# Attention with routed and dense MLPs: value tiles with places of their own in the plan, first loads put ahead of the decay sums

## The chip, the cores and the metric

One core of a Trainium2 chip runs the whole program. The metric is the device time of one execution in microseconds, as a median over runs; the profile is one further execution, recorded by the hardware profiler, with its own time beside it.

## What is computed

The reference, cut to what matters here: causal attention over 4 batches of 8 heads, 576 positions and 64 columns a head, with a decay that is a running sum of `max(s, 0)`; its output is the input of a top-1 mixture of 8 experts, and that of a dense two-layer network.

```python
scores = scale * np.matmul(q, k.transpose(0, 1, 3, 2))
cum = np.cumsum(np.maximum(s, 0.0), axis=-1)
bias = -(cum[:, :, :, None] - cum[:, :, None, :])
scores = np.where(causal, -1000000000.0, scores + np.minimum(bias, 0.0))
attn = np.exp(scores - np.max(scores, axis=-1, keepdims=True))
attn = attn / (np.sum(attn, axis=-1, keepdims=True) + 1e-09)
attn_out = np.matmul(attn, v)                  # then rows of 8 x 64 = 512
y = gate_w * (np.maximum(x @ w1[e], 0) @ w2[e])  # e: the expert of a row's largest logit
h = y @ w_in; out = (h * np.clip(h + 3, 0, 6) / 6) @ w_out
```

## The kernel before

**Parts in time.** The attention part comes first, then ten passes of expert products, then the dense network in steps. All three are one instruction stream for each engine. Only the attention part is touched by the change.

**Attention.** A unit is one block of 128 queries of one batch (the fifth block of a batch has 64), a pair is two heads of a unit. 80 pairs run one after the other in a software pipeline: in one slot, TensorE makes the scores of the next pair (`sp`, L575), VectorE adds the decay and finds the minimum (`ne`, L588), ScalarE takes the exponential (`pp`, L594), TensorE turns the pair before (`pt`, L603), ScalarE and VectorE split it into two float16 halves (`hi`, L624, and `lo`, L625), and TensorE multiplies the pair before that with the value tile (`o`, L658). A full unit has four pairs with two exponentials each, the fifth unit of a batch four pairs with one, so a batch has 36 exponentials.

**Inputs of a batch.** q and k come in three chunks of 256, 256 and 64 positions (`load`), are lined up by GpSimd (`xs`), turned by TensorE (`pk`, L490) and split. Values come as five tiles of 128 positions (`load_v`: two DMAs of 128 KB, into `v32`, of which there are two buffers). `v_part` makes the two halves of a value tile: a copy by ScalarE (L514), a scaling and a subtraction by GpSimd (L445 and L516), into `vbuf[b % 2][j]`; the buffers of batch b are those of batch b - 2. The decay sums `cum` are made once for all batches in 32 rows (L395 to L405), written to DRAM (`cum_d`, L407), and read back spread over 128 partitions (`load_cum`, tile `cp`). For heads 0 to 3 of the first unit, TensorE spreads the sums instead (`first_cum`, tile `pf`).

**What sets the order.** All loads are issued by SyncE (SP), one after the other; a load that waits for a buffer holds back all that stand behind it. `then` chains the first loads in the written order. Everything later is put into slots of the pair pipeline by `at_time`, on a scale where a pair costs 1.0 to 2.9 (`price`); the whole plan is 158.4 units long. For each chunk a due time is worked out backwards (`due`), and all its work is put there: the loads of its value tiles at the start, then the turns of k and q, then its value parts. Inside each engine a scheduler places an instruction by its own model of when the operands are there; `issue_after` fixes that one instruction is behind another.

**What else uses the engines there.** From batch 2 on, the first expert weights are loaded through the same staging buffers (`wf`, in turn in the `k32` and `q32` buffers) and split by GpSimd and ScalarE (L249 to L251). After a unit its rows are split (`xw`, L687 and L688) and stored (`x_d`, L690 and L695), and after a batch its tokens are scattered (`tok_d`, L804). `fold_cum` (`cp`, L445) copies sums for the fifth units and for the last batch.

## Time and profile before

| what | value |
|---|---|
| median of 3 runs | 871.22 us (870.36 to 875.09) |
| profiled execution, its own time | 872.09 us |
| its span from first to last instruction | 870.3 us |
| TensorE busy in the span | 794.4 us (91%) |
| ScalarE, GpSimd busy | 461.7 us, 296.4 us |
| ScalarE waiting for value tiles | 15.2 us up to 70 us, 4.2 us up to 140, 1.8 us up to 200 |
| last value products of the attention | at 272 us |

The span runs from the first to the last instruction; the 1.8 us between it and the execution's time lie around it. The profiled execution is 0.9 us above the median.

### The profile page before, as it was taken

The numbers are of one execution on the slowest core, as the hardware profiler recorded it, in microseconds if no ns is written. First come the engines' busy times: TensorE is split into PE (matmuls) and PEld (weight loads), VectorE is DVE, ScalarE is ACT, GpSimd is POOL, SyncE is SP. The second block draws the span as 40 slices with busy tenths as digits, with TensorE's granted clock in tenths as the row PEclk, the third lists the DMA queues.
The fourth block names the chain that finished last, engine by engine and source line by source line (L and its number), as shares of the span: only waits on it lengthen the run. The fifth ranks groups of instructions, "written<-read, shape, count | busy, mean of one in ns | idle before, by whom it ended". The sixth has DMA issues, their size and how long they took to land.

```text
span 870.3 us, 21871 instructions
## 1 busy us (share of the span) xinstructions
PE 794.4 (91%) x8340; PEld 659.7 (76%) x8340; DVE 623.5 (72%) x1542; ACT 461.7 (53%) x854; POOL 296.4 (34%) x402
## 2 busy tenths in 40 slices
PE   5888788888888998899999999999999999999993
PEld 4567567666667897566778888888888888888882
DVE  4677777866767645789879569988677777777770
ACT  3677767867875433666656343554444344443440
POOL 2565663868984225044331100000022022211232
PEclk8799999999999999999999999999999999999997
DMA  7957245243613678988887355654444545444420
GB/s 165 262 130 214 70 89 180 51 96 101 178 47 79 171 209 219 321 304 273 256 259 270 98 170 165 220 174 158 141 148 129 159 150 162 142 141 153 153 95 27
DMA packets 154327, 142.03 MB, mean 163 GB/s; under 512 B 68710, under 2 KB 122214, under 8 KB 153446
## 3 DMA queue, kind: packets, MB, share of 16 engines
q1 hardware_dynamic: 150422, 130.50, 50.2%
q0 software_dynamic: 3792, 10.06, 3.5%
q8 instruction: 67, 1.10, 0.5%
q14 instruction: 46, 0.38, 0.2%
HBM read 106.70 MB, written 28.54 MB: 155 GB/s over the span
## 4 chain that ended last, share of the span: by engine, by line
PE 48%; DMA 17%; DVE 10%; POOL 7%; ACT 5%; issue 5%; SPq 4%; another core or an unknown queue 1%; POOLq 0%; ACTq 0%; DVEq 0%
PE bank L1350 18%; PE py L1241 8%; PE bank L1267 8%; PE ph L1130 7%; DMA wf<-in_moe_w_dram 5%; DMA v<-in_v_dram 3%; PE pt L603 2%; PE sp L575 2%; PE o L658 2%; DVE wo L1110 2%; DMA t_d<-cl 2%; DMA xsT<-xg 1%; DMA t_d<-sets 1%; ACT pp L594 1%; SPq L215 1%
## 5 line engine op out<-in xcount | busy, mean ns | idle before, releaser
L1267 PE MATMUL bank<-x2T,wi 128*128 128x256 f16 x1728 | 193.5, 273 | 0.9 <-POOL x2T L1249 0.6
L1267 PEld LDWEIGHTS <-wi 128*128 128x128 f16 x1728 | 169.1, 98 | 21.0 <-issue 1.5
L1350 PE MATMUL bank<-wo,sets 128*128 128x256 f16 x1512 | 170.2, 273 | 1.2 <-DVE sets L1279 0.7
L1350 PEld LDWEIGHTS <-sets 128*128 128x128 f16 x1512 | 147.7, 98 | 19.0 <-DVE sets L1279 1.0
L1278 ACT ACTIVATE sets<-back 128x896 f16<-128x896 f32 x72 | 68.1, 950 | 91.9 <-PE bank L1350 74.7
L1130 PE MATMUL ph<-xsT,t 128*128 128x224 f16 (+7 forms) x960 | 109.6, 276 | 3.6 <-DVE hT L1135 3.6
L1241 PE MATMUL py<-hT,t 128*128 128x224 f16 (+7 forms) x960 | 108.4, 273 | 4.2 <-DVE hT L1135 2.3
L1361 POOL TENSOR_TENSOR u<-sa 128x256 f32<-128x256 f32 x9 | 9.3, 1035 | 296.4 <-ACT sa L1360 296.4
L1130 PEld LDWEIGHTS <-t 128*128 128x128 f16 x960 | 86.8, 99 | 24.1 <-issue 4.2
L1241 PEld LDWEIGHTS <-t 128*128 128x128 f16 x960 | 85.5, 98 | 25.7 <-issue 5.7
L1279 DVE SCALAR_TENSOR_TENSOR sets<-back,sets 128x896 f16<-128x896 f32 x72 | 80.2, 1119 | 22.1 <-ACT sets L1278 21.9
L625 DVE SCALAR_TENSOR_TENSOR lo<-pt,hi 128x256 f16<-128x256 f32 (+3 forms) x144 | 72.8, 519 | 28.5 <-ACT hi L624 27.4
L257 DVE SCALAR_TENSOR_TENSOR t<-wf,t 128x1024 f16<-128x1024 f32 x53 | 66.7, 1258 | 28.6 <-ACT t L254 27.9
L658 PE MATMUL o<-v,hi 128*128 128x65 f16 (+2 forms) x960 | 63.0, 201 | 24.9 <-ACT hi L624 17.9
L603 PE MATMUL pt<-idf,pp 128*128 128x128 f32 (+1 forms) x400 | 77.9, 310 | 7.5 <-DVE kT L499 1.9
L624 ACT ACTIVATE hi<-pt 128x256 f16<-128x256 f32 (+3 forms) x144 | 64.1, 460 | 35.4 <-PE pt L603 27.0
L594 ACT ACTIVATE pp<-ne,nm 128x128 f32<-128x128 f32 (+4 forms) x144 | 76.9, 580 | 0.6 <-DVE nm L588 0.6
L254 ACT ACTIVATE t<-wf 128x1024 f16<-128x1024 f32 x53 | 55.5, 1053 | 36.1 <-DMA wf<-in_moe_w_dram 36.1
L588 DVE CUSTOM_DVE_ANT_0 ne<-sp,cp 128x128 f32<-128x128 f32 (+4 forms) x144 | 61.2, 456 | 16.5 <-ACT pp L594 11.4
L658 PEld LDWEIGHTS <-hi 128*128 128x128 f16 (+2 forms) x960 | 47.9, 104 | 32.3 <-ACT hi L624 21.0
L603 PEld LDWEIGHTS pt<-idf,pp 128*128 128x128 f32 (+1 forms) x400 | 46.9, 152 | 17.5 <-issue 3.6
L1249 POOL TENSOR_TENSOR x2T<-y,x2T 128x360 f32 (+5 forms) x24 | 20.8, 871 | 111.1 <-ACT x2T L1248 97.4
(206 smaller groups left out, 1263.4 us busy)
## 6 DMA issues: line engine op xcount, KB each, us to landing
wf<-in_moe_w_dram SPq DMA_DIRECT2D x64, 512.0 KB
back<-t_d SPq DMA_DIRECT2D x144, 128.0 KB
wd<-in_moe_w_in_dram SPq DMA_DIRECT2D x16, 512.0 KB
wd<-in_moe_w_out_dram SPq DMA_DIRECT2D x16, 512.0 KB
cp<-cum_d SPq DMA_DIRECT2D x6, 1152.0 KB
t_d<-cl SPq DMA_DIRECT2D x24, 256.0 KB
t_d<-sets SPq DMA_DIRECT2D x24, 256.0 KB
t_d<-wo SPq DMA_DIRECT2D x24, 256.0 KB
```

Source lines behind the costliest of these rows:

```text
L257: stt(out=lo, in0=fv, scalar=sc, in1=hi, op0=ALU.mult, op1=ALU.subtract)
L594: mark["act"] = nc.scalar.activation(self.view(self.pp, e), self.view(self.ne, e), AF.Exp, bias=self.nm[:, e:e + 1], scale=-1.0).ins
L603: nc.tensor.transpose(self.pt[g][:m, x, :], src, idf)
L624: nc.scalar.activation(hi, pt, AF.Copy, scale=SP)
L625: stt(out=lo, in0=pt, scalar=SP, in1=hi, op0=ALU.mult, op1=ALU.subtract)
L658: mark["pe"] = nc.tensor.matmul(dst, a, x, start=first, stop=last).ins
L1130: mark["pe"] = nc.tensor.matmul(ph[:, :n], wt[c][:, a, cols], xT[:, KD * b_ + c, :n], start=(c == 0 and x == 0), stop=(c == KD - 1 and x = ...
L1241: nc.tensor.matmul(py[:, :rows], wt2[:, j_, f, cols], hT[i_][:, f, :rows], start=(f == 0 and x == 0), stop=(f == KF - 1 and x == 2),)
L1267: m = nc.tensor.matmul(dst, wi[:, a, kk, fs], x2[:, KD * b_ + kk], start=(kk == 0 and x == 0), stop=(kk == KD - 1 and x == 2),)
L1278: nc.scalar.activation(hi, t, AF.Copy, scale=SG)
L1279: stt(out=lo, in0=t, scalar=SG, in1=hi, op0=ALU.mult, op1=ALU.subtract)
L1350: m = nc.tensor.matmul(banks[k_][:, :HM], sets[:, s % 4, a, k_], w_sums[f][:, b_, k_], start=(f == 0 and x == 0), stop=(f == HO - 1 and x ...
```

## The change

It changes four things in the attention part.

- `load_v(0, 0)` and `load(0, 1)`, the first value tile and the second chunk of q and k, are issued ahead of the decay sums. The write of the sums to `cum_d` moves from SyncE's queue to ScalarE's.
- `first_cum` is called for both halves of the heads, so TensorE spreads the first 128 sums of all eight heads, and ScalarE makes two copies instead of one. The two loads of sums that opened the chain (4 heads by 256, 4 heads by 128) become one of 8 heads by columns 128 to 256.
- A value part leaves its chunk's list. `v_part` is now placed by itself: for the first two chunks of a batch behind the turns, for the third chunk at 8.5 units into its batch, and for the last batch at times of a table `v_last`, counted from the start of the batch before. Its load stands 3 units ahead of it, and its ScalarE copy is fixed behind the last exponential written before it.
- The sums of batches 1 to 3 are loaded behind the last store of rows that is written before them (`mark["x"]`).

```diff
-        with tc.issue_after(ahead[0]):
-            cum_out = nc.sync.dma_start(cum_d, cum_sb)
+        last = [ahead[0]]
+
+        def then(f, *args):
+            with tc.issue_after(last[0]):
+                last[0] = f(*args).ins
+
+        then(load_v, 0, 0)
+        then(load, 0, 1)
+        nc.scalar.dma_start(cum_d, cum_sb)
...
-        def first_cum():
+        def first_cum(h0):
...
-            pc = psT.tile([128, FIRST, 128], F32, tag="T", name="pf")
-            for h in range(FIRST):
+            pc = psT.tile([128, H // 2, 128], F32, tag="T", name="pf")
+            for h in range(H // 2):
                 nc.tensor.matmul(
-                    pc[:, h], idf[:BH, h:h + 1].to_broadcast([BH, 128]),
+                    pc[:, h], idf[:BH, h0 + h:h0 + h + 1].to_broadcast([BH, 128]),
...
-            nc.scalar.activation(cums[0][:, :FIRST, :128], pc, AF.Copy)
+            nc.scalar.activation(cums[0][:, h0:h0 + H // 2, :128], pc, AF.Copy)
...
+        def v_part(b, j):
+            def f():
+                m = R[j]
+                v32 = loaded.pop((b, j, "v"))
+                vt = vbuf[b % 2][j]
+                with tc.issue_after(mark["act"]):
+                    nc.scalar.activation(vt[:m, :, 0:D], v32[:m], AF.Copy, scale=SV)
+                hi16(v32[:m], v32[:m], SV)
+                gtt(out=vt[:m, :, D + 1:], in0=v32[:m], in1=vt[:m, :, 0:D], op=ALU.subtract)
+            return f
...
-        then(load_cum, 0, slice(FIRST, H), 0, 256)
-        then(load_cum, 0, slice(0, FIRST), 128, 256)
-        then(load_v, 0, 0)
-        then(load, 0, 1)
+        then(load_cum, 0, slice(0, H), 128, 256)
         then(load_v, 0, 1)
...
+        v_last = (4.5, 6.5, 22.0, 24.0, 26.0)
...
             at_time(t0, begin)
-            for j in range(CH[c][0] // 128, CH[c][0] // 128 + (2 if c < 2 else 1)):
-                at_time(t0, lambda b=b, j=j: load_v(b, j))
+            nt = 4 if c < 2 else 2
+            for x, j in enumerate(range(CH[c][0] // 128, CH[c][0] // 128 + (2 if c < 2 else 1))):
+                if b + 1 == B:
+                    tv = start_of(NCH * (b - 1)) + v_last[j]
+                elif c == 2:
+                    tv = start_of(NCH * b) + 8.5
+                else:
+                    tv = t0 + (nt + x) * per
+                at_time(tv - 3.0, lambda b=b, j=j: load_v(b, j))
+                at_time(tv, lambda j=j, hold=hold: hold[j]())
             at_time(t0, next_load)
...
+                    def late_cum(b=b, x=x):
+                        with tc.issue_after(mark["x"]):
+                            load_cum(b, slice(H // 2 * x, H // 2 * x + H // 2))
+
+                    at_time(t0 + x * per, late_cum)
```

The order of SyncE's queue at the start of the program, before, from the write of the sums to the third value tile (`k_223` and `q_222` are the second chunk, `v_219`, `v_226`, `v_235` the first three value tiles, `wgf` the gate's weights):

```order
L407 DMA cum_d<-cum_sb 32x576
L414 DMA cp<-cum_d 128x4x256
L414 DMA cp<-cum_d 128x4x128
L341 DMA v_219<-in_v_dram 64x8x64 x2
L329 DMA k_223<-in_k_dram 128x8x128
L329 DMA q_222<-in_q_dram 128x8x128
L341 DMA v_226<-in_v_dram 64x8x64 x2
L897 DMA wgf_101<-in_moe_w_gate_dram 128x4x8
L897 DMA wgf_102<-in_moe_w_gate_dram 64x2x8 x4
L414 DMA cp<-cum_d 128x8x320
L341 DMA v_235<-in_v_dram 64x8x64 x2
L414 DMA cp<-cum_d 128x2304 x2
```

The same stretch of SyncE's queue after the change (`v_215`, `v_225`, `v_234`, `v_237` are the value tiles 0 to 3):

```order
L341 DMA v_215<-in_v_dram 64x8x64 x2
L329 DMA k_219<-in_k_dram 128x8x128
L329 DMA q_218<-in_q_dram 128x8x128
L421 DMA cp<-cum_d 128x8x128
L341 DMA v_225<-in_v_dram 64x8x64 x2
L410 DMA wgf_101<-in_moe_w_gate_dram 128x4x8
L410 DMA wgf_102<-in_moe_w_gate_dram 64x2x8 x4
L421 DMA cp<-cum_d 128x8x320
L341 DMA v_234<-in_v_dram 64x8x64 x2
L341 DMA v_237<-in_v_dram 64x8x64 x2
```

The first value tile and the second chunk have moved to the head, and the sums of batch 1 (`128x2304 x2`, 2.36 MB) have left the place between value tiles 2 and 3.

ScalarE's order in the same stretch, before, from the fifth exponential on (the L514 rows are the copies of value tiles 0, 1 and 2):

```order
L594 ACTIVATE pp<-ne,nm 128x128
L514 ACTIVATE v_0_185<-v_219 128x8x64
L594 ACTIVATE pp<-ne,nm 128x128
L514 ACTIVATE v_1_187<-v_226 128x8x64
L498 ACTIVATE kT<-pk 128x2x256
L624 ACTIVATE hi<-pt 128x256
L594 ACTIVATE pp<-ne,nm 128x128 x2
L503 ACTIVATE xs<-pk 128x512
L624 ACTIVATE hi<-pt 128x256
L594 ACTIVATE pp<-ne,nm 128x256 x2
L514 ACTIVATE v_2_189<-v_235 128x8x64
```

ScalarE's order in the same stretch, after the change, from the first exponentials to the fourth value tile (the L458 rows are the copies of value tiles):

```order
L600 ACTIVATE pp<-ne,nm 128x128 x4
L458 ACTIVATE v_0_185<-v_215 128x8x64
L514 ACTIVATE qT<-pk 128x512
L514 ACTIVATE kT<-pk 128x2x256
L630 ACTIVATE hi<-pt 128x256 x2
L600 ACTIVATE pp<-ne,nm 128x128 x2
L458 ACTIVATE v_1_187<-v_225 128x8x64
L600 ACTIVATE pp<-ne,nm 128x128
...
L514 ACTIVATE kT<-pk 128x2x256
L630 ACTIVATE hi<-pt 128x256
L600 ACTIVATE pp<-ne,nm 128x256 x2
L458 ACTIVATE v_2_189<-v_234 128x8x64
L519 ACTIVATE xs<-pk 128x512
L458 ACTIVATE v_3_191<-v_237 128x8x64
```

Before, the copies of tiles 0, 1, 2 and 3 stood behind 5, 6, 10 and 16 exponentials; now they stand behind 4, 6, 12 and 12. Later, the five copies of batches 1 to 3 stood behind 24, 26, 30, 30 and 32; 42, 42, 50, 52 and 56; and 78, 78, 86, 88 and 92 exponentials. Now they stand behind 32, 33, 38, 42 and 52; 68, 69, 74, 78 and 88; and 82, 86, 100, 100 and 104.

GpSimd's order in batch 2, before, where the tokens of batch 1 are scattered and the first expert weights are split (`cp` is `fold_cum`, `wf` and `t` are the weight split, `xs` and `qT` belong to chunks of batch 3):

```order
L804 DMA tok_d<-what,pos_s 5120x3 x5
L445 TENSOR_SCALAR cp<-cp 64x576 x3
L249 TENSOR_SCALAR wf<-wf 128x1024
L251 TENSOR_TENSOR t_3949<-wf,t_3949 128x1024
L688 TENSOR_TENSOR xw<-xr,xw 128x512
L445 TENSOR_SCALAR xs<-k_3535 128x4x2x64
L445 TENSOR_SCALAR xs<-q_3534 128x4x2x64
L445 TENSOR_SCALAR qT<-xs 128x512
```

The same place on GpSimd after the change:

```order
L810 DMA tok_d<-what,pos_s 5120x3 x5
L450 TENSOR_SCALAR cp<-cp 64x576 x2
L450 TENSOR_SCALAR v_3696<-v_3696 128x512
L450 TENSOR_SCALAR cp<-cp 64x576
L450 TENSOR_SCALAR v_3699<-v_3699 128x512
L460 TENSOR_TENSOR v_2_199<-v_3696,v_2_199 128x8x64
L460 TENSOR_TENSOR v_3_201<-v_3699,v_3_201 128x8x64
L249 TENSOR_SCALAR wf<-wf 128x1024
L694 TENSOR_TENSOR xw<-xr,xw 128x512
L450 TENSOR_SCALAR xs<-k_3555 128x4x2x64
L450 TENSOR_SCALAR xs<-q_3554 128x4x2x64
L450 TENSOR_SCALAR v_3780<-v_3780 64x512
```

Three value parts of the last batch now stand between the scatter and the weight splits; before, they were done earlier in batch 2.

## Rows read from the trace of the kernel before

**Rows 1.** The page: span, and busy tenths and granted clock in 40 slices.

```profile
span 870.3 us, 21871 instructions
PE   5888788888888998899999999999999999999993
PEclk8799999999999999999999999999999999999997
```

**Rows 2.** ScalarE's waits (total us, times, longest), from 0:70, 70:140 and 140:200 us.

```profile
ACT v L514 <- DMA v<-in_v_dram: 15.2, 8, 4.3
...
ACT v L514 <- DMA v<-in_v_dram: 4.2, 1, 4.2
...
ACT v L514 <- DMA v<-in_v_dram: 1.8, 1, 1.8
```

**Rows 3.** Timeline of ScalarE: value tiles 0 to 2, exponentials 11 and 12.

```profile
17.60 0.64 ACT L514 ACTIVATE v<-v 128x512 f16<-128x512 f32 x1 [3.35 <-DMA v<-in_v_dram]
...
22.82 0.64 ACT L514 ACTIVATE v<-v 128x512 f16<-128x512 f32 x1 [4.29 <-DMA v<-in_v_dram]
...
31.41 0.64 ACT L514 ACTIVATE v<-v 128x512 f16<-128x512 f32 x1 [3.25 <-DMA v<-in_v_dram]
...
32.69 0.90 ACT L594 ACTIVATE pp<-ne,nm 128x256 f32<-128x256 f32 x2
```

**Rows 4.** Timeline of SyncE's issues at the start: start, us to issue, what.

```profile
7.80 0.33 SPq L407 DMA_DIRECT2D cum_d<-cum_sb  x1
9.47 0.92 SPq L414 DMA_DIRECT2D cp<-cum_d  x2
10.44 1.41 SPq L341 DMA_DIRECT2D v<-in_v_dram  x2
...
18.15 3.93 SPq L897 DMA_DIRECT2D wgf<-in_moe_w_gate_dram  x5
...
24.96 1.26 SPq L414 DMA_DIRECT2D cp<-cum_d  x2
```

**Rows 5.** Windows: length, busy PE, PEld, DVE, ACT, POOL; clock, DMA share, GB/s.

```profile
4.00:6.00 2.00, 2.00 (x7) 1.23 (x8) 1.93 (x6) 0.60 (x1) 0.18 (x1) 1.00 0.93 210
8.00:10.00 2.00, 2.00 (x16) 1.51 (x14) 0.69 (x1) 1.50 (x3) 0.00 (x0) 1.00 0.16 37
18.00:26.00 8.00, 5.32 (x38) 3.50 (x37) 1.94 (x7) 2.98 (x8) 4.29 (x8) 0.50 0.77 155
94.00:98.00 4.00, 1.37 (x19) 0.92 (x18) 1.33 (x6) 0.17 (x1) 3.46 (x10) 1.00 0.55 117
200.00:220.00 20.00, 16.06 (x268) 12.21 (x266) 12.88 (x51) 16.27 (x36) 19.47 (x21) 0.91 0.30 83
350.00:370.00 20.00, 16.61 (x105) 10.12 (x104) 16.96 (x25) 13.45 (x19) 0.00 (x0) 1.00 1.02 315
```

**Rows 6.** Waits of all engines from 92 to 104 us.

```profile
PE o L658 <- ACT hi L624: 3.8, 1, 3.8
```

**Rows 7.** Instructions on value tiles up to 275 us: ns minimum, median, maximum.

```profile
L514 ACT ACTIVATE v<-v x20: 625/637/641, 17.6 to 167.6; 128x512 f16<-128x512 f32 x16, 64x512 f16<-64x512 f32 x4
L445 POOL TENSOR_SCALAR v<-v x20: 607/617/621, 18.4 to 168.3; 128x512 f32<-128x512 f32 x16, 64x512 f32<-64x512 f32 x4
L516 POOL TENSOR_TENSOR v<-v,v x20: 1116/1127/1134, 19.8 to 169.0; 128x512 f16<-128x512 f32 x16, 64x512 f16<-64x512 f32 x4
```

**Rows 8.** Timeline of GpSimd from 185 to 200 us, its rows with idle time.

```profile
185.01 1.94 POOL L445 TENSOR_SCALAR cp<-cp 64x576 f32<-64x576 f32 x3 [4.35 <-DVE nm L588]
...
189.88 2.13 POOL L251 TENSOR_TENSOR t<-wf,t 128x1024 f16<-128x1024 f32 x1 [1.17 <-ACT t L250]
...
199.37 1.04 POOL L249 TENSOR_SCALAR wf<-wf 128x1024 f32<-128x1024 f32 x1 [2.02 <-DMA wf<-in_moe_w_dram]
```

**Rows 9.** The chain that ended last: start us, us, what.

```profile
7.80 1.65 DMA cum_d<-cum_sb
...
93.81 4.51 DMA v<-in_v_dram
...
272.46 1.64 PE o L658 x48
```

**Rows 10.** SyncE's queue up to 275 us: its longest waits in total.

```profile
SPq L690 <- POOL xw L688: 22.7, 8, 7.6
```

More of the change, by code (lines that the diff above doesn't have):

```diff
@@ L507, in turn @@
                 return [line_up, flip]
-            def v_part(j):
-                def f():
-                    m = R[j]
-                    v32 = loaded.pop((b, j, "v"))
-                    vt = vbuf[b % 2][j]
-                    nc.scalar.activation(vt[:m, :, 0:D], v32[:m], AF.Copy, scale=SV)
-                    hi16(v32[:m], v32[:m], SV)
-                    gtt(out=vt[:m, :, D + 1:], in0=v32[:m], in1=vt[:m, :, 0:D], op=ALU.subtract)
-                return f
-            vs = [v_part(t0 // 128 + j) for j in range(nr)]
+            vs = [v_part(b, t0 // 128 + j) for j in range(nr)]
             groups = ((0, 1), (2, 3)) if big else (range(NP),)
@@ L889, in start_of @@
             return begins[NP * place[u] + p]
-        last = [cum_out.ins]
-        def then(f, *args):
-            with tc.issue_after(last[0]):
-                last[0] = f(*args).ins
-        then(load_cum, 0, slice(FIRST, H), 0, 256)
-        then(load_cum, 0, slice(0, FIRST), 128, 256)
-        then(load_v, 0, 0)
-        then(load, 0, 1)
+        then(load_cum, 0, slice(0, H), 128, 256)
         then(load_v, 0, 1)
@@ L909 @@
         then(load, 0, 2)
-        at_slot(-1, first_cum)
+        for h0 in (0, H // 2):
+            at_slot(-1, lambda h0=h0: first_cum(h0))
         for x, fs in enumerate(prep(0, 0, fast=True)):
@@ L934, in begin @@
                 hold["f"] = prep(b, c)
+            hold.update((j, v_part(b, j)) for j in range(NCH))
             def next_load(g=g):
@@ L940 @@
             at_time(t0, begin)
-            for j in range(CH[c][0] // 128, CH[c][0] // 128 + (2 if c < 2 else 1)):
-                at_time(t0, lambda b=b, j=j: load_v(b, j))
+            nt = 4 if c < 2 else 2
[8 more added lines that the diff above has]
+                at_time(tv, lambda j=j, hold=hold: hold[j]())
             at_time(t0, next_load)
-            for x in range(6 if c < 2 else 3):
-                for y in range(2 if x < (4 if c < 2 else 2) else 1):
+            for x in range(nt):
+                for y in range(2):
                     at_time(t0 + (x + 1.3 * y) * per, lambda x=x, y=y, hold=hold: hold["f"][x][y]())
@@ L948 @@
                 for x in range(2):
-                    at_time(t0 + x * per, lambda b=b, x=x: load_cum(b, slice(H // 2 * x, H // 2 * x + H // 2)))
+                    def late_cum(b=b, x=x):
+                        with tc.issue_after(mark["x"]):
+                            load_cum(b, slice(H // 2 * x, H // 2 * x + H // 2))
+                    at_time(t0 + x * per, late_cum)
         def fill_tables():
```

1 line of the change is left out of this document (removed).

## The prediction

> **What bounds the kernel now.** I read the page's slices first. TensorE is at 5 to 8 tenths in the first twelve, which are the attention part, and at 8 or 9 in all behind them but the last [rows 1]; the last value products start at 272 us [rows 9]. So the expert and dense parts have little idle time to give, and the change doesn't touch them: what it is worth is how much earlier the attention part ends, and whether the rest moves up with it.
>
> In the attention part no engine is full. The pairs go round from TensorE to VectorE to ScalarE and back, and a wait of one of them for something outside the ring stops all three. The waits of ScalarE, by stretch, show such an outside wait: the copy of a value tile waits for its load for 15.2 us up to 70 us, 4.2 us up to 140 and 1.8 us up to 200 [rows 2], 21.2 us together. The timeline shows how: the copies of tiles 0, 1 and 2 stand in front of exponentials and wait 3.35, 4.29 and 3.25 us [rows 3]. That the ring stops is seen in batch 1: from 94 to 98 us ScalarE is busy for 0.17 of 4 us, TensorE for 1.37 [rows 5], and TensorE's own wait for that one stop is 3.8 us [rows 6]. The chain that ended last agrees: it runs through the write of the sums at 7.80 us and through a value load of 4.51 us at 93.81 [rows 9].
>
> Why the loads are late: SyncE issues nothing between the first q and k and the end of the sums, 7.80 us, then waits for that write to land, until 9.47 [rows 4]. From 8 to 10 us the DMA engines are busy for 0.16 of the time [rows 5]. The first value tile is issued only at 10.44, behind two loads of sums [rows 4].
>
> **The start of batch 0.** By 8 us the first q and k are in, since the DMA engines are idle then. Now the transfers can go on without the hole. Ahead of value tile 2, counted from the diff and the order, lie tile 0 (0.26 MB), the second q and k (1.05), sums (8 x 128 columns x 128 rows x 4 bytes, 0.52), tile 1 (0.26), the gate's weights, sums (8 x 320 columns, 1.31), and tile 2 itself (0.26): 3.66 MB. The 256-byte rows of the first q and k moved at 210 GB/s [rows 5]; that is 17.4 us, and I add 1 us for the gate's small rows, of whose 3.93 us of issue [rows 4] most lies beside transfers (an estimate). Tile 2 then lands at 8 + 17.4 + 1 = 26.4 us. Without the three waits, ScalarE would be through its twelfth exponential, which ended at 32.69 + 0.90 = 33.6 [rows 3], at 33.6 - 10.9 = 22.7, less the copy of tile 2 (0.6), which stood ahead of it, plus the second copy of `first_cum` (0.6, taken from the copy of a value tile, which has as many columns [rows 7]): 22.7. So it waits again, 3.7 us, for tile 2, and is through the copy at 27.0 instead of 33.6. **Gain: 6.6 us.** Tile 3 lands 1.2 us behind tile 2, and the copies of tile 2 and of `xs` fill that. The bounds: at the pace of the trace between the issue of the first sums, 9.47, and the landing of tile 1, 22.82 [rows 3, 4], 2.36 MB in 13.35 us or 177 GB/s, tile 2 lands at 29.7 and the gain is 3.3. With no wait at all it is 10.3. I take the middle one, since its row is the same kind of transfer with nothing in the way.
>
> The write of `cum_d` from ScalarE's queue costs that engine one issue, 0.33 us on SyncE [rows 4]; it stands where ScalarE waits for TensorE's first sums, so I count nothing, and the 0.33 if that cover is gone. Four more spreading products lie on TensorE in a stretch in which ScalarE has the longer work; they take the place of a load, and I count nothing (bounds: 0 and 0.6 us, one more copy's length).
>
> **The rest of batch 0.** Of the 15.2 us, 4.3 lie behind tile 2. Part of them came from the sums of batch 1 (two loads issued at 24.96 [rows 4]), which stood ahead of tile 3 and are now late. TensorE is busier here, so that some of a stop is caught up afterwards; I take half. **Gain: 2.2 us**, bounds 0 and 4.3.
>
> **Batch 1 and batch 2.** Their value tiles were copied a batch ahead, as soon as the buffers were free, with the load right ahead of the copy. Now the load stands 3 units ahead. The plan of 158.4 units ends at 272 us [rows 9], so 3 units are some 5 us, and the load took 4.51 us from issue to landing [rows 9]. That is enough, narrowly. For batch 1, I take TensorE's wait, **3.8 us** [rows 6] (bounds: 2.6, which is what TensorE lacked from 94 to 98, and 4.2); for batch 2, half of 1.8, **0.9 us** (bounds 0 and 1.8).
>
> **The last batch.** Its tiles 2, 3 and 4 move on GpSimd to behind the scatter of batch 1's tokens, among the first weight splits. Each is 0.62 + 1.13 us [rows 7], 5.2 together. GpSimd had idle time there: 4.35, 1.17 and 2.02 us [rows 8]; the first of these lies ahead of the place. Right behind it GpSimd is full, 19.47 of 20 us from 200 to 220 [rows 5], and the weight splits hold the staging buffers of the last chunks. Of the other two idle times, 3.2 us, most can hide work. I take half of the 5.2 as **loss: 2.6 us** (bounds 0 and 5.2). ScalarE's share, three copies of 0.64, is moved, not added.
>
> **The rest of the program** moves up as it is: the weight loads are put at slots of the pairs and come earlier with them. I count no loss; the price if that fails is a rival below.
>
> **Sum:** 6.6 + 2.2 + 3.8 + 0.9 - 2.6 = 10.9 us. Against the profiled execution, 870.3 of span and 1.8 around it, 872.1 - 10.9 = 861.2. That execution is 0.9 above the median of the runs shown; I forecast **861 us**, 1.2% below that median. 0.5% (4.4 us) is about what a measurement of this kernel can tell from no change: 866.9 and 875.6 are the lines.
>
> **Rivals.**
>
> *The clock holds.* From 18 to 26 us the granted clock is 0.50, the lower level of 1.2 GHz, after TensorE had stood still behind the first wait, and TensorE's 5.32 us there [rows 5] would be 2.7 at 2.4 GHz. If the early waits vanish and the clock stays up, the first term is 10.3 instead of 6.6 and 2.7 us come on top: 861 - 6.4 = 855 us. For it: the hole in the transfers is real. Against it: 3.66 MB have to come through. The Trainium skill ("TensorE: Matmul & The Clock Gate", "HAM oscillation — how this bites in real kernels") says that waits for DMA throw the array back to its half clock, and that keeping it fed avoids this; the row agrees on the fall. By that rule this rival would be the rule rather than the exception; I hold that a wait of 3.7 us remains.
>
> *The transfers bound the start.* The order changes, the bytes don't, and what waited for tile 0 and 1 now waits for the second q and k, the sums and tiles 2 and 3. At 177 GB/s the first term is 3.3, the second 0, and with GpSimd's 5.2 in full: 3.3 + 3.8 + 0.9 - 5.2 = 2.8, or 869 us.
>
> *The loads come too late (slower).* A value load is now some 5 us ahead of its copy, and ScalarE's copy can't slide behind later exponentials. In SyncE's queue it stands behind stores of rows, which wait for GpSimd: 22.7 us in 8 waits, up to 7.6 at once [rows 10]. Each store that is waited for makes the tiles behind it late, and their copies stop the ring. There are 15 such tiles in batches 1 to 3; a mean wait of 0.73 us eats the 10.9 us, that is the point from which it decides. At 1.8 us each it is 861 + 15 x 1.8 - 10 (waits would overlap with what these batches lose anyway, an estimate) = 878 us. Against it: before, with loads right ahead of the copies, only 6 us were lost in those batches [rows 2].
>
> *Given back by the experts.* From 350 to 370 us the DMA engines are full (share 1.02, 315 GB/s) and TensorE is busy for 16.61 of 20 us [rows 5]. If the weights bound that stretch from a fixed start, an earlier attention part buys nothing: 871 us. Against it: their loads begin at slots of the pairs.
>
> **How the numbers follow.** Chances: forecast 0.50 (own range 856 to 867), clock 0.20, transfers 0.15, late loads 0.10, given back 0.05. The range leaves out the late loads, the given-back case above 870 and the far end of the clock case: **853 to 870**. Faster by over 0.5%: forecast and clock, and the part of the transfers case in which only one of its bounds is met, 0.75. Within 0.5%: the rest of that case and the given-back case, 0.15. Slower: 0.10.
>
> **What would show it.** After the change: no wait of ScalarE for value tiles 0 and 1, and one of some 3 to 4 us for tile 2, near 23 us; none at 94 us; DMA busy from 8 to 10 us; the last value products of the attention near 261 us; GpSimd's work on value tiles among the weight splits, with the stretch behind as full as before. I am wrong if ScalarE's waits for value tiles in batches 1 to 3 grow past 10 us, if TensorE waits for the second k in the first 20 us for more than 3 us, or if the attention part ends earlier and the end of the program doesn't.

## The result, and the profile after the change

The changed kernel takes **882.13 us** (median of 4 runs, 878.99 to 882.55) beside 870.79 us before (median of 4, 868.65 to 875.09): ratio **1.0116**, 95% interval 1.0071 to 1.0161. It is slower by about 10 us where 10 us less were forecast. The profiled execution took 878.99 us, 877.3 of them span, and is the fastest of the four; the others have spans of 880.3 to 880.8.

The page's slices of the changed kernel: span, TensorE's busy tenths, granted clock.

```profile
span 877.3 us, 21901 instructions
...
PE   7888977957797998899999999999999999999993
...
PEclk9999999977597999999999999999999999999997
```

The start is better than before [rows 1]. Slices 9 to 11 (175 to 241 us) are worse: TensorE falls to 5 tenths in the first of them and the granted clock to 5 in the last. So the gain came, and something behind it took more than all of it.

**The start did what it should.** ScalarE's waits for value tiles, from 0:70 us and from 140:210 (70:140 has none; total us, times, longest):

```profile
ACT v L458 <- DMA v<-in_v_dram: 3.4, 2, 3.2
...
ACT v L458 <- DMA v<-in_v_dram: 13.6, 2, 10.0
```

The 15.2 us of before up to 70 us [rows 2] are 3.4, the 4.2 behind them are gone, and the 1.8 of the last stretch have become 13.6. The timeline of ScalarE's copies of tiles 0 to 3 shows the first part (start, duration, what, in brackets the idle time before it):

```profile
14.34 0.62 ACT L458 ACTIVATE v<-v 128x512 f16<-128x512 f32 x1
...
18.09 0.64 ACT L458 ACTIVATE v<-v 128x512 f16<-128x512 f32 x1
...
27.42 0.64 ACT L458 ACTIVATE v<-v 128x512 f16<-128x512 f32 x1 [3.23 <-DMA v<-in_v_dram]
...
28.71 0.64 ACT L458 ACTIVATE v<-v 128x512 f16<-128x512 f32 x1 [0.18 <-DMA v<-in_v_dram]
```

Two waits of [rows 3] are gone and the third is there, 3.23 us. SyncE's queue issues three loads in the hole of [rows 4]. It stands from 8.35 to 11.81 us instead, until the write of the sums has landed; the columns are start, us to issue, what:

```profile
5.60 1.41 SPq L341 DMA_DIRECT2D v<-in_v_dram  x2
7.05 0.62 SPq L329 DMA_DIRECT2D k<-in_k_dram  x1
7.72 0.63 SPq L329 DMA_DIRECT2D q<-in_q_dram  x1
11.81 0.37 SPq L421 DMA_DIRECT2D cp<-cum_d  x1
```

**Where it was lost.** I followed the attention part by its 20 units (5 query tiles in each of 4 batches), by the end of ScalarE's division copy `xw` of each, start plus duration. For unit 13 (counted from 1) it is 189.71 + 0.61 = 190 us before and 170.96 + 0.64 = 172 after. The expectations below number units 13 to 17 in the same way, and call the last one unit 19. The ends of some units, of one profiled execution each and in whole us, and after minus before:

| unit | 5 | 10 | 13 | 14 | 15 | 17 | 20 |
|---|---|---|---|---|---|---|---|
| before | 89 | 154 | 190 | 207 | 217 | 237 | 276 |
| after | 80 | 139 | 172 | 198 | 216 | 245 | 284 |
| difference | -9 | -15 | -18 | -9 | -1 | +8 | +8 |

The changed kernel is 18 us ahead at unit 13, and 8 behind at unit 17. The 26 us go at the seam from batch 2 to batch 3. Behind the attention little changes: span less the end of unit 20 is 595 us before and 593 after.

The seam, first in GpSimd's timeline: the last of the five scatters of batch 1's tokens, and what stands behind it.

```profile
167.21 0.92 POOL L810 DMA_INDIRECT tok_d<-what,pos_s  x1 [0.30 <-issue]
176.89 1.31 POOL L450 TENSOR_SCALAR cp<-cp 64x576 f32<-64x576 f32 x2 [8.76 <-DMA tok_d<-what,pos_s]
178.28 0.62 POOL L450 TENSOR_SCALAR v<-v 128x512 f32<-128x512 f32 x1
...
179.74 0.62 POOL L450 TENSOR_SCALAR v<-v 128x512 f32<-128x512 f32 x1
180.32 2.21 POOL L460 TENSOR_TENSOR v<-v,v 128x512 f16<-128x512 f32 x2
```

GpSimd's next instruction, a copy of sums, waits 8.76 us until the scatter has landed; before, the same place waited 4.35 [rows 8]. It is this copy that waits, and not GpSimd behind every scatter: behind the last issue of batch 2's scatter the next instruction begins at once. Why the copy waits I don't know, and no run takes it away from there.

```profile
254.98 0.92 POOL L810 DMA_INDIRECT tok_d<-what,pos_s  x1 [0.30 <-issue]
255.89 0.24 POOL L820 TENSOR_TENSOR acc<-acc,oh 64x8 f16<-64x8 f16 x1
```

The last batch's value tiles 2 and 3 stand behind it and hold their buffers until the first is through, at 181.4. Tile 4 needs one of them. SyncE's queue shows the load, and what was issued just before the scatter, two late loads of sums, 2.36 MB:

```profile
160.79 0.93 SPq L421 DMA_DIRECT2D cp<-cum_d  x2
...
166.25 1.42 SPq L239 DMA_DIRECT2D wf<-in_moe_w_dram  x1
181.47 0.61 SPq L343 DMA_DIRECT2D v<-in_v_dram  x1
```

The queue stands from 167.7 to 181.5 us. And ScalarE, which has the copy of tile 4 in the middle of its exponentials:

```profile
173.68 0.59 ACT L514 ACTIVATE kT<-pk 128x512 f16<-128x512 f32 x1
184.26 0.64 ACT L458 ACTIVATE v<-v 64x512 f16<-64x512 f32 x1 [9.99 <-DMA v<-in_v_dram]
```

The chain that ended last goes through the write of the sums, which lands 4.00 us after its issue instead of 1.65 [rows 9], and through both scatters that met late sums (start, us, what); in [rows 9] there was a value load in their place.

```profile
7.80 4.00 DMA cum_d<-cum_sb
...
103.51 8.60 DMA tok_d<-what,pos_s
...
167.21 9.46 DMA tok_d<-what,pos_s
```

What follows is slow as well. Windows of 20 us (length, busy PE, PEld, DVE, ACT, POOL, granted clock, DMA share, GB/s):

```profile
180.00:200.00 20.00, 11.68 (x148) 9.37 (x147) 9.04 (x30) 12.34 (x21) 19.88 (x22) 0.67 0.34 106
200.00:220.00 20.00, 16.00 (x213) 12.01 (x212) 10.13 (x40) 11.12 (x26) 17.77 (x19) 0.76 0.27 82
220.00:240.00 20.00, 15.21 (x120) 9.26 (x118) 8.88 (x35) 13.63 (x27) 15.46 (x18) 0.50 0.46 150
```

GpSimd is full from 180 to 200 with what it could not do during its wait. TensorE, which stood for 8 of these 20 us, is granted 0.67, and from 220 to 240 us 0.50, the lower level of 1.2 GHz; before it had 0.91 in each of these three windows ([rows 5] has the middle one). At the upper level its 15.21 us from 220 to 240 would be 7.6 (an estimate from that row), so the clock may be a part of what is lost here. The chain that ended last says less for it: from 177 to 265 us it is on GpSimd for 53 us and on TensorE for 2 (before, 41 and 8).

### The profile page after: what moved, and what is told of

Read it like the earlier page. It is cut to its first block, busy times and chain, and to the rows that moved or that the text cites. A ratio compares the mean times of both kernels' runs of the same rounds, so it can differ in the third digit from the quotient of the medians.

```text
span 877.3 us, 21901 instructions
## 1 busy us (share of the span) xinstructions
PE 796.3 (91%) x8348; PEld 661.0 (75%) x8348; DVE 621.8 (71%) x1542; ACT 462.0 (53%) x855; POOL 293.8 (33%) x402
## 4 chain that ended last, share of the span: by engine, by line
PE 57%; DMA 13%; POOL 9%; DVE 7%; ACT 5%; issue 4%; SPq 3%; POOLq 0%; ACTq 0%; DVEq 0%
PE bank L1282 21%; PE bank L1365 17%; PE py L1256 7%; PE ph L1145 7%; DMA wf<-in_moe_w_dram 6%; DMA tok_d<-what,pos_s 2%; POOL t L251 2%; PE pt L609 2%; PE o L664 2%; DVE ne L594 2%; SPq L215 1%; DVE lo L631 1%; ACT pp L600 1%; ACT hi L630 1%; POOL tok_d L810 1%
## 5 line engine op out<-in xcount | busy, mean ns | idle before, releaser
L1145 PEld LDWEIGHTS <-t 128*128 128x128 f16 x960 | 85.2, 98 | 26.6 <-issue 6.6
L1256 PEld LDWEIGHTS <-t 128*128 128x128 f16 x960 | 85.3, 98 | 23.9 <-issue 4.0
L609 PE MATMUL pt<-idf,pp 128*128 128x128 f32 (+1 forms) x400 | 76.1, 308 | 14.3 <-ACT xs L519 8.0
```

The costliest lines, as they stand in the source:

```text
L609: nc.tensor.transpose(self.pt[g][:m, x, :], src, idf)
L1145: mark["pe"] = nc.tensor.matmul(ph[:, :n], wt[c][:, a, cols], xT[:, KD * b_ + c, :n], start=(c == 0 and x == 0), stop=(c == KD - 1 and x = ...
L1256: nc.tensor.matmul(py[:, :rows], wt2[:, j_, f, cols], hT[i_][:, f, :rows], start=(f == 0 and x == 0), stop=(f == KF - 1 and x == 2),)
```

## Experiments

The theories, as the expectations name them. **T1:** the late sums of the last batch meet the scatter, GpSimd waits for it 4 us longer, and value tiles, staging buffers and SyncE's queue are late with it. **T2:** the place of the last batch's value tiles behind the scatter is what costs, whatever the sums do. **T3:** the new order of work is slow in the last batches by itself. **T4:** T1 and T2 add up. **T5:** GpSimd's amount of work from the scatter on bounds the seam. **T6:** ScalarE's instructions that wait for GpSimd stand at fixed pairs, so that a lead turns into waits there. **T7:** something that none of these orders touches bounds the seam.

All ratios are to the kernel before, on the same chip in the same rounds. The table has the results; "scatter" is GpSimd's wait for it in front of the copies of sums at 173 to 185 us (in before, `e3_cum`, `e10_fold`, `e14_gather_split` and `e15_all_gather_split` the row names VectorE as what came last), "for GpSimd" all that ScalarE waited for GpSimd from 160 to 275 us, "clock" the mean granted clock from 160 to 285 us, "rest" the span less the end of unit 20. All but the ratio is of one profiled execution, on chips where the median of the kernel before lies between 869.6 and 875.4 us; that of `e8_both` is the fastest of its 12 and 7.5 us below their median.

| kernel | ratio (95%) | unit 13 | unit 14 | unit 17 | unit 20 | scatter | for GpSimd | clock | rest |
|---|---|---|---|---|---|---|---|---|---|
| before | 1 | 190 | 207 | 237 | 276 | 4.4 | 6.2 | 0.92 | 595 |
| after | 1.0116 (1.0071-1.0161) | 172 | 198 | 245 | 284 | 8.8 | 8.3 | 0.77 | 593 |
| e1_head | 0.9949 (0.9922-0.9975) | 187 | 204 | 233 | 273 | 4.5 | 5.8 | 0.93 | 594 |
| e2_tail | 1.0215 (1.0188-1.0242) | 182 | 204 | 252 | 290 | 6.7 | 10.7 | 0.80 | 602 |
| e3_cum | 0.9997 (0.9973-1.0021) | 181 | 205 | 242 | 277 | 5.6 | 6.1 | 0.90 | 595 |
| e4_last | 1.0101 (1.0078-1.0124) | 178 | 201 | 250 | 285 | 8.4 | 14.9 | 0.81 | 600 |
| e5_cum12 | 1.0087 (1.0056-1.0117) | 174 | 196 | 241 | 280 | 4.8 | 20.1 | 0.86 | 599 |
| e6_both12 | 0.9997 (0.9969-1.0024) | 178 | 200 | 232 | 275 | 5.0 | 13.1 | 0.89 | 601 |
| e7_both1 | 1.0004 (0.9975-1.0034) | 176 | 197 | 229 | 273 | 5.2 | 13.4 | 0.87 | 600 |
| e8_both | 0.9969 (0.9938-0.9999) | 177 | 199 | 235 | 272 | 5.1 | 9.8 | 0.86 | 593 |
| e9_head_late1 | 1.0017 (0.9986-1.0049) | 179 | 195 | 227 | 274 | 4.7 | 17.8 | 0.89 | 599 |
| e10_fold | 1.0019 (0.9988-1.0050) | 179 | 202 | 235 | 274 | 4.2 | 15.0 | 0.88 | 597 |
| e11_late1_fold | 1.0101 (1.0050-1.0151) | 179 | 208 | 249 | 285 | 4.9 | 13.9 | 0.82 | 599 |
| e12_both_fold | 1.0103 (1.0052-1.0153) | 179 | 207 | 240 | 280 | 4.3 | 14.0 | 0.88 | 597 |
| e13_gather | 1.0013 (0.9991-1.0035) | 179 | 196 | 228 | 271 | 5.0 | 14.0 | 0.88 | 597 |
| e14_gather_split | 1.0017 (0.9996-1.0038) | 182 | 198 | 231 | 273 | 4.8 | 13.6 | 0.88 | 599 |
| e15_all_gather_split | 1.0067 (1.0043-1.0091) | 177 | 198 | 230 | 271 | 3.9 | 9.8 | 0.89 | 600 |
| e16_head_gather_split | 0.9969 (0.9943-0.9995) | 181 | 198 | 227 | 268 | 4.6 | 10.9 | 0.93 | 599 |

### The two halves, and one part of the second undone at a time

`e1_head` is the kernel before with the head of the diff alone:

```diff
+        then(load_v, 0, 0)
+        then(load, 0, 1)
+        nc.scalar.dma_start(cum_d, cum_sb)
...
+        then(load_cum, 0, slice(0, H), 128, 256)
...
+        for h0 in (0, H // 2):
+            at_slot(-1, lambda h0=h0: first_cum(h0))
```

> The kernel before with the head part of the change alone: value tile 0 and the second q and k loaded ahead of the sums, the sums written from ScalarE's queue, first sums of all heads by TensorE. The plan of batches 1 to 3 is that of before. Theory T1 (the late sums of the next batch meet the scatter, GpSimd's value parts stand behind it) and T2 (the place of the last batch's value tiles) agree here: what the head gains stays, some 8 to 9 us (batch 0 ends 9 us earlier in the changed kernel), so 861 to 864 us. If the gain is given back somewhere in the plan whatever the later tiles do (T3: the weight splits of batch 3 fall in a slower order once the attention moves up), it is 867 to 875 us and batch 3 takes 75 us or more from first to last exponential instead of 67.

`e2_tail` is the changed kernel with these lines as they were.

> The changed kernel with its head part undone: what is left are the new places of the value tiles and the sums of batches 1 to 3 behind the marked instruction. T1 and T2: the loss in batch 2's last unit and batch 3 stays (some 19 us), the gain at the start of batch 0 goes (9 us), the gain in batch 1 (4 us) stays: 885 to 892 us. T3: without the head the last batches fall back to the order of before, and the loss shrinks: 868 to 876 us.

The head alone gains 0.5% (4.5 us, 2.2 to 6.8), half of what T1 and T2 expected, and the profiled execution keeps most of it: 5 us ahead at unit 1, 5 at unit 5, 3 at unit 13, 2 at unit 20. The rest alone loses 2.15%, 18.7 us. So T3's idea that the lead makes the loss is out: without the head the loss is there in full.

`e3_cum` loads the sums when their slot comes:

```diff
-                        with tc.issue_after(mark["x"]):
-                            load_cum(b, slice(H // 2 * x, H // 2 * x + H // 2))
+                        load_cum(b, slice(H // 2 * x, H // 2 * x + H // 2))
```

> The changed kernel, but the sums of batches 1 to 3 are loaded when their slot comes and not behind the marked instruction. T1: the scatter of the tokens no longer shares the DMA engines with 2.36 MB of sums, GpSimd's wait for it at 177 us falls from 8.8 to about 4 us, ScalarE's wait of 10 us for tile 4 of the last batch falls below 4 us, and 10 to 18 us come back: 862 to 870 us. T2: the tiles still stand behind the scatter, at most 4 us come back: 875 to 880 us. T3: nothing comes back, 878 to 883 us. If the early sums push back value tiles 2 and 3 of batch 0, up to 4 us of that are lost again.

`e4_last` puts the last batch's tiles ahead of the scatter:

```diff
-        v_last = (4.5, 6.5, 22.0, 24.0, 26.0)
+        v_last = (4.5, 6.5, 10.5, 12.5, 14.5)
```

> The changed kernel with the last batch's value tiles 2, 3 and 4 put ahead of the scatter of batch 1's tokens (plan units 10.5, 12.5, 14.5 instead of 22, 24, 26). T2: the wait of 10 us for tile 4 vanishes, SyncE's queue is not held at 168 to 181 us, and most of the 19 us come back: 862 to 868 us. T1: the wait for tile 4 vanishes too, but GpSimd's wait of 8.8 us for the scatter stays and makes the sums and weight splits behind it late: 5 to 10 us come back, 870 to 876 us. T3: 876 to 883 us, batch 3 still takes 75 us or more.

The sums alone give back 10 us (1.0116 to 0.9997), the low end of what T1 said. The edit does more than it says: ScalarE's order of instructions differs from the changed kernel's from 27 us on. ScalarE's waits for value tiles from 160 us on fall to 1.1 us, and GpSimd's wait is 5.60 us again (timeline, `e3_cum`; the row names VectorE as what came last):

```profile
173.54 0.92 POOL L810 DMA_INDIRECT tok_d<-what,pos_s  x1 [0.30 <-issue]
180.06 1.31 POOL L450 TENSOR_SCALAR cp<-cp 64x576 f32<-64x576 f32 x2 [5.60 <-DVE lo L631]
```

The tiles alone give back nothing (1.0101), which neither T1 nor T2 expected, and the time is at the upper end of what T3 said: the wait of 9.99 us is gone, but the scatter's 8.44 stays (GpSimd's timeline, `e4_last`),

```profile
182.57 1.95 POOL L450 TENSOR_SCALAR cp<-cp 64x576 f32<-64x576 f32 x3 [8.44 <-DMA tok_d<-what,pos_s]
```

and ScalarE waits for GpSimd at the next instruction that needs it, the split of an expert weight (ScalarE's timeline, `e4_last`):

```profile
187.97 1.06 ACT L250 ACTIVATE t<-wf 128x1024 f16<-128x1024 f32 x1 [5.62 <-POOL wf L249]
...
224.52 1.06 ACT L250 ACTIVATE t<-wf 128x1024 f16<-128x1024 f32 x1 [4.07 <-POOL wf L249]
```

So tile 4's wait was only the first thing to be late. What is behind GpSimd takes its place.

### Which sums, and both parts together

`e5_cum12` keeps only batches 1 and 2 late, `with tc.issue_after(mark["x"]) if b < 3 else ExitStack()`. `e6_both12` adds the `v_last` of `e4_last`, `e7_both1` has only batch 1 late (`b == 1`), and `e8_both` none.

> The changed kernel, but only the sums of batches 1 and 2 stay behind the marked instruction; those of batch 3, the last, are loaded when their slot comes. By the ends of the 20 units (ScalarE's division copies), the changed kernel was 18 us ahead of the one before at unit 13 (172 against 190) and lost 26 us over units 14 to 17; with all sums early it was 9 us ahead there and lost 14. T1 (what loses is the load of the last batch's sums meeting the scatter): 9 us ahead or more at unit 13, at most 3 lost behind it, 860 to 866 us. T4 (two causes that add up: that load, some 12 us, and the place of the last batch's value tiles behind the scatter, some 13): 18 ahead at unit 13, 13 lost, 866 to 872 us. If the late sums are not what loses (T3): 880 us and more.

> As e5_cum12, and the last batch's value tiles 2 to 4 ahead of the scatter (plan units 10.5, 12.5, 14.5). T4: both causes are gone, the lead of 14 to 18 us at unit 13 stays to the end: 854 to 862 us. T1: the tiles cost nothing where they stand, so the same as e5_cum12 within 3 us, 860 to 866 us. T3: 870 us or more.

> As e6_both12, but the sums of batch 2 come early too; only batch 1's are late, those that would be loaded in the first 40 us, when the DMA engines are full. If the lead comes from that one load (some 4 us in batch 0) and the sums of batch 2 meet the scatter of batch 0's tokens (GpSimd waited 7.9 us for it in the changed kernel, 4 before), this is 2 to 4 us faster than e6_both12. If the late sums of batch 2 gained, it is 2 to 5 us slower.

> The changed kernel with all sums early and the last batch's value tiles ahead of the scatter; with the changed kernel (late sums, tiles behind), e3_cum (early, behind) and e4_last (late, ahead) it makes a table of two by two. T4: the place of the tiles is worth some 8 to 13 us where the sums are early, though it was worth nothing where they were late: 862 to 867 us. T1: the place is worth nothing here either, 873 to 877 us.

Two by two: sums late, tiles behind 1.0116; late, ahead 1.0101; early, behind 0.9997; early, ahead 0.9969. The sums are worth 10 and 12 us, the tiles 1 and 2, the latter within the intervals. By batches the picture is less simple. With the tiles behind the scatter, taking back batch 3's sums alone gives only 2.5 us (`e5_cum12`; by T1 and T4 it would have been 10 or more); with the tiles ahead it gives 9 (`e4_last` to `e6_both12`). In the same rounds the place of the tiles is worth 8 us (`e5_cum12` to `e6_both12`). So with the sums of batches 1 and 2 late, either cause is enough for most of the loss, and T4's plain sum is wrong as well; the times of `e5_cum12` and `e6_both12` (883.0 and 875.6 us, where the kernel before had 875.4) lie where T3 put them. Batch 3's sums alone were late in no run. The scatter itself is clear in the table: 8.8, 6.7 and 8.4 us in the three kernels with batch 3's sums late, 3.9 to 5.6 in the fifteen others. The first scatter, of batch 0's tokens at 98 to 113 us, shows the same: GpSimd waits 7.4 to 8.0 us behind it in the five kernels in which batch 2's sums are issued beside it, and 2.4 to 6.3 in the thirteen others. But there it costs nothing that the time shows: with batch 2's sums early, the one step from `e6_both12` to `e7_both1`, the ratio goes from 0.9997 to 1.0004. So the longer wait is not yet a loss; what stands behind it decides.

No kernel went below the head alone, though these four are 12 to 16 us ahead at unit 13. At unit 20 they are between 4 us ahead and 4 behind.

### What eats the lead

`e9_head_late1` is `e1_head` with batch 1's sums late, and no new places of value tiles. `e10_fold`, `e11_late1_fold` and `e12_both_fold` are `e1_head`, `e7_both1` and `e8_both` with the last batch's copies of sums by `nc.vector.tensor_scalar` instead of GpSimd's.

> The head part alone (as e1_head, value tiles of batches 1 to 3 as before), and the sums of batch 1 alone behind the marked instruction. In the kernels with new places for the value tiles the late sums of batch 1 brought some 4 us of lead in batch 0, and all of the lead above 3 to 4 us was gone at the end of the attention part. If the places of the value tiles are what costs it, the lead stays here: unit 13 ends 7 us or more ahead of before, and the time is 4 us below e1_head, ratio 0.988 to 0.992. T5 (GpSimd, full from the scatter of batch 1's tokens on, is what an earlier attention part runs into, whatever brings it forward): the lead at unit 13 is larger than in e1_head but at unit 19 it is 3 to 4 us again, ratio 0.994 to 0.999.

> As e1_head, with the last batch's copies of sums (eight of 64 x 576, 5.79 us in one piece on GpSimd at 198 to 211 us in all kernels so far) by VectorE, which is busy for 13 of 20 us there. T5: GpSimd bounds batch 3, so some 3 to 5 us are gained behind unit 14, ratio 0.988 to 0.991. If GpSimd isn't what bounds there, VectorE's share of the ring grows and it is the same or up to 5 us slower, ratio 0.995 to 1.000.

> As e7_both1 (batch 1's sums late, all new places ahead of the scatter; 14 us ahead at unit 13, 3 at the end), with the last batch's copies of sums by VectorE. T5: the lead that was lost at unit 14 and at units 18 and 19 stays in part, 5 us or more below e7_both1, ratio 0.990 to 0.995. Otherwise within 2 us of it, ratio 0.998 to 1.003.

> As e8_both (all sums early, new places ahead of the scatter), with the last batch's copies of sums by VectorE. T5: 4 to 6 us below e8_both, ratio 0.990 to 0.993. Otherwise within 2 us of it, ratio 0.995 to 0.999.

T5's forecasts are missed: with 5.79 us less work on GpSimd all three are slower, by 6 to 12 us against their pairs (0.9949 to 1.0019, 1.0004 to 1.0101, 0.9969 to 1.0103). That doesn't rule T5 out, for which the chain speaks, 53 of 88 us on GpSimd in the changed kernel. The work went to VectorE, which has a part in every pair: the eight copies take it 7.1 us in `e10_fold`, and in `e12_both_fold` ScalarE waits 6.99 us for VectorE at 206 us. `e9_head_late1` is 11 us ahead at unit 13, 9 at unit 17 and 2 at unit 20, near the 3 to 4 that T5 said, but its time lies above both forecasts; it loses 7 us in one unit. GpSimd's timeline there: the scatter of batch 2's tokens, the gather of the first expert's rows, which needs it, and behind the gather a step of the gate:

```profile
238.56 0.92 POOL L809 DMA_INDIRECT tok_d<-what,pos_s  x1 [0.30 <-issue]
...
246.17 1.02 POOL L204 DMA_INDIRECT xg<-x_d,slots  x1 [2.18 <-DMA slots<-tok_d]
...
248.78 0.30 POOL L752 TENSOR_SCALAR eq<-ex 128x16 f32<-128x16 f32 x1
```

ScalarE has the gate's exponential in line, and its pairs' work behind that:

```profile
238.36 0.77 ACT L599 ACTIVATE pp<-ne,nm 128x576 f32<-128x576 f32 x1
249.11 0.21 ACT L758 ACTIVATE ex<-ex 128x16 f32<-128x16 f32 x1 [9.99 <-POOL eq L752]
...
253.10 0.63 ACT L692 ACTIVATE xw<-xr 128x512 f16<-128x512 f32 x1 [0.98 <-DVE xr L676]
```

The gather stood ahead of the gate's step before the change, too; there ScalarE waited 1.2 us for it (ScalarE's timeline, before):

```profile
255.60 0.63 ACT L687 ACTIVATE xw<-xr 128x512 f16<-128x512 f32 x1 [1.09 <-DVE xr L671]
...
259.46 0.22 ACT L753 ACTIVATE ex<-ex 128x16 f32<-128x16 f32 x1 [1.16 <-POOL eq L747]
```

From the first issue of the scatter to the gather it takes 12.9 us here and 12.4 before. What differs is ScalarE's order: before, the gate's exponential stands behind 136 of the pairs' exponentials and behind the unit's division copy, here behind 134 and ahead of that copy. So a part of this wait comes from where the scheduler put it. In `e6_both12` and `e7_both1` it stands behind 136, as before, and ScalarE waits 7.2 and 6.9 us all the same. That is T6, and the last four kernels try it. `e13_gather` is `e9_head_late1` with

```diff
-                at_time(routed + 14.5, lambda: ([load_slots(p) for p in range(NS)], got0.extend(gather(0))))
-                at_time(routed + 19.0, lambda: xs0.append(turn(0, got0)))
+                at_time(routed + 14.5, lambda: [load_slots(p) for p in range(NS)])
+                at_time(routed + 19.5, lambda: got0.extend(gather(0)))
+                at_time(routed + 24.0, lambda: xs0.append(turn(0, got0)))
```

and the three behind it also have `at_slot(n + 5, lambda x=x: splits[x]())` for `n + 3`: `e14_gather_split` on `e9_head_late1`, `e15_all_gather_split` on `e7_both1`, `e16_head_gather_split` on `e1_head`. In the traces no split moves by that: `e14_gather_split` has the order of `e13_gather` on every engine and in SyncE's queue, so the two are one program, and the other two test the gather alone.

> As e9_head_late1 (head part, sums of batch 1 late), with the gather of the first expert's rows 5 plan units later, so that on GpSimd it stands behind the gate's steps of the next group instead of ahead of them. T6: ScalarE's wait of 9.99 us for the gate's step vanishes, the lead of 8 to 10 us that e9_head_late1 had at unit 17 stays to unit 19, and the time falls by 5 to 9 us, ratio 0.991 to 0.997. T7: the wait turns up at another place, ratio 1.000 to 1.004.

> As e13_gather, and each split of the first expert's weights two pairs later behind its load. T6: the waits of ScalarE for GpSimd's share of the splits (4.9 and 2.9 us) go as well, another 2 to 5 us, ratio 0.987 to 0.994. T7: no change against e13_gather, or slower, since the staging buffers are held longer.

> As e7_both1 (the whole change, but only batch 1's sums late and the last batch's value tiles ahead of the scatter; 14 us ahead at unit 13), with both moves of e14_gather_split. T6: 8 us or more of the lead reach unit 19, ratio 0.988 to 0.994. T7: 0.998 to 1.004.

> As e1_head (ratio 0.9949; ScalarE waits 5.8 us for GpSimd at 160 to 275 us, as in the kernel before), with both moves. T6: nothing to gain, within 2 us of e1_head, ratio 0.993 to 0.998. If it gains 5 us or more, the two moves are good by themselves and don't tell of the lead.

In `e13_gather` the gate's step is ahead of the gather, 3.8 us earlier than in `e9_head_late1`:

```profile
245.03 0.30 POOL L752 TENSOR_SCALAR eq<-ex 128x16 f32<-128x16 f32 x1
...
247.78 1.07 POOL L204 DMA_INDIRECT xg<-x_d,slots  x1 [0.72 <-DMA slots<-tok_d]
```

ScalarE's wait falls from 9.99 to 5.13 us. Unit 20 ends at 271 instead of 274, about as much as two executions of one order differ (`e14_gather_split`: 273). `e16_head_gather_split` keeps its lead over the seam, 9 us at unit 13 and 8 at unit 20, but its order is that of `e1_head` up to 246 us, so the move didn't make the lead; from unit 13 to 20 before takes 85 us, `e1_head` 86, `e16_head_gather_split` 87 and the others 91 to 113. So of T6's mechanism one wait is shown. Its price is not: the time stays (1.0017 to 1.0013), as T7 said, and `e15_all_gather_split` is even slower, 1.0067 against 1.0004. What is gained up to unit 20 is missing behind it: the rest is 597 to 602 us in thirteen kernels, and 593 to 595 only in before, after, `e1_head`, `e3_cum` and `e8_both`. Of these few us the waits show a part, a stop of TensorE in the dense part for a weight of the second dense matrix, which before, after, `e1_head` and `e8_both` do not have beyond 0.3 us (TensorE's waits from 580 to 680 us, `e9_head_late1`):

```profile
PE bank L1351 <- DVE wo L1276: 2.8, 1, 2.8
```

Why that weight is late there I don't know. So T6 holds for one wait at a place that I moved, and T7 can't be ruled out for the rest.

A rival that none of T1 to T7 names is TensorE's clock. In the table, before, `e1_head` and `e16_head_gather_split`, which take 85 to 87 us from unit 13 to 20, have 0.92 or 0.93 from 160 to 285 us; the five that take 106 us or more (after, `e2_tail`, `e4_last`, `e5_cum12`, `e11_late1_fold`) have 0.77 to 0.86, the ten between them 0.86 to 0.90. A wait that stops TensorE and the lower level behind it come together here. Against the clock as the main cause stands the chain of the changed kernel, which is hardly on TensorE; no run tells how the loss divides.

## Why the prediction was wrong

- **The start of batch 0** (6.6 us). Mechanism right: no wait for tiles 0 and 1, one for tile 2 of 3.23 us (3.7 forecast), its copy through at 28.06 (27.0 forecast), so 5.5 us instead of 6.6, DMA busy from 8 to 10 us (0.80 instead of 0.16). Of the write of the sums I counted the issue; that it lands after 4.00 us instead of 1.65, with the new loads ahead of it, I did not. With **the rest of batch 0** (2.2) the forecast is 8.8 us up to unit 5; the profile shows 9, and that is luck in part, since the second term had to bring more than forecast for it. As a change by itself the head was worth 4.5 us of time.
- **The clock.** From 18 to 26 us the granted clock is 0.80 and not 0.50 [rows 5], so part of the rival "the clock holds" came true there. Later the clock took it back: 0.67 from 180 to 200 us and 0.50 from 220 to 240. The Trainium skill ("TensorE: Matmul & The Clock Gate", "HAM oscillation — how this bites in real kernels") expects the fall where TensorE waits for data. The trace agrees at 180 us, where TensorE is busy for 1.88 of the 8 us from 176 to 184 while the value tile is late; from 220 to 240 it is busy for 15.21 of 20 us, and no such wait is plain.
- **Batches 1 and 2** (4.7 us). From unit 5 to unit 13 the lead grew from 9 to 18 us, twice what was forecast, and the stop at 94 us is gone. How much of this the new places made isn't shown, since before is one execution: `e1_head`, `e10_fold` and `e16_head_gather_split` have the old places and one order up to 192 us, all are 5 or 6 us ahead at unit 5, and they are between 3 and 12 ahead at unit 13.
- **The last batch** (loss 2.6). Mis-sized, and by the wrong mechanism. I counted GpSimd's 5.2 us of work and looked for idle time to hide it. What counted was that these steps stand behind a copy of sums that waits for the scatter to land, that they hold the buffer which tile 4's load needs, and that SyncE's queue and ScalarE's order stand behind that load. The place costs 1 to 8 us, by what else is late (`e4_last`, `e8_both`, `e6_both12`).
- **The late sums: the step that failed.** The prediction has them only as a gain, where tile 3 no longer stands behind them. Of the 1.15 MB loads of batches 2 and 3 I never asked what they would then stand beside. They met the scatter, which a copy of sums on GpSimd waits for, and all that stands behind that copy: 8.76 us instead of 4.35. Loading all sums at their slot again gives 10 to 12 us, the whole loss against before. How much of that goes through the scatter is less sure: batch 3's sums, which meet the one at the seam, give back 2.5 us by themselves with the tiles behind it and 9 with the tiles ahead, and batch 2's, which meet the first one, nothing.
- **"The rest of the program moves up as it is"** failed too. Every kernel that came to unit 13 more than 4 us early lost half of its lead or more before unit 20, but for `e16_head_gather_split`. ScalarE's waits for GpSimd grow there from 6 us to as much as 20 (though not in `e3_cum`, which loses its lead with 6.1), the granted clock is below before's in all of them, and most lose 2 us or more behind unit 20. So the kernel without the two losing parts, `e8_both`, gains no more than the head alone; which of these takes its lead is not shown.
- **The rivals.** "The loads come too late" gave 878 us and came nearest, with a chance of 0.10; its test, waits for value tiles of more than 10 us in batches 1 to 3, was met at 13.6. Its mechanism was not what happened: not 15 tiles by 1.8 us behind stores of rows, but one tile by 10.0, behind GpSimd. That its number came near is luck.

What stays open: how the loss divides between the sums of batches 1 and 2 and those of batch 3 (2.5 or 9 us by the place of the tiles), why the copy of sums waits for the scatter, whether GpSimd's work bounds the seam, what the clock's share is, and what makes the rest behind unit 20 longer.

The best kernel here is the head alone, `e1_head`, 0.5% below the kernel before; `e8_both` and `e16_head_gather_split` (0.3% below) can't be told from it.

## What to carry to other kernels

A transfer that is moved is to be priced where it goes as well as where it leaves: list what else is in flight there, and which engine waits for that with its queue. A load moved out of a crowded start is worth little if it lands beside a small transfer that a whole queue of instructions waits for.

And a lead is not yet a gain: here several kernels came 12 to 16 us earlier to unit 13 and none of them ended earlier by more than the head alone. Before counting a gain at the front as a gain at the end, follow the places at which an engine waits for another's transfer (here scatter, landing, gather), and ask whether those move up too.

## What the runs showed of the hardware

Five scatters from GpSimd's queue (160 packets, 0.01 MB in that queue's row of the transfers) were waited for 3.9 to 5.6 us after the last was issued in fifteen kernels, and 6.7 to 8.8 us in the three in which 2.36 MB of sums were issued from SyncE's queue at the same moment; the scatter of batch 0's tokens 2.4 to 6.3 and 7.4 to 8.0 us. The write of the sums, 0.07 MB, landed after 1.65 us before and after 4.00 in the changed kernel, where it is in another queue and 1.3 MB of loads are issued just ahead of it. That a small transfer can take twice as long beside large ones of another queue I had not expected. The Trainium skill ("DMA: Bandwidth & Descriptors", "Issuing engines are not separate DMA queues") says that transfers of all issuing engines run on the same 16 DMA engines and interleave; the longer waits fit that.

One program doesn't take the same time twice in its parts. `e13_gather` and `e14_gather_split` have the same order on every engine, and their units end up to 3 us apart. `e10_fold` has the order of `e1_head` on every engine up to 192 us, where its edit begins, and ends unit 8 at 115 us against 123. Of the 8 us, 3.1 go at the copy of a value tile, which waited 1.61 us in `e10_fold`, and 2.6 at a wait that has 1.29 us there and whose cause the profile doesn't name (ScalarE's timeline, `e1_head`):

```profile
93.80 0.64 ACT L519 ACTIVATE v<-v 128x512 f16<-128x512 f32 x1 [4.74 <-DMA v<-in_v_dram]
...
115.00 0.49 ACT L629 ACTIVATE hi<-pt 128x384 f16<-128x384 f32 x1 [3.86 <-remote]
```

So a lead of a few us at one unit, read from one execution of each kernel, can't be put down to the edit between them; the ratios, from 4 to 12 executions, can carry more.
